# One reload moved forward in an in-order DMA queue: an mLSTM cell followed by a squared-ReLU feed-forward block

## The chip, the cores and the metric

The kernel runs on one core of one Trainium2 chip. The metric is the device time of one execution in microseconds. Faster or slower needs 2%.

## The reference, cut to what matters

```
for t in range(S):                       # 768 steps, 4 x 8 heads of 40
    m_new = max(f_t + m, i_t); C = f*C + i * v_t k_t^T; n = f*n + i*k_t
    y_t = sigmoid(o_t) * (C q_t) / max(|n . q_t|, 1)
x = y as (3072, 320)
out = relu(x @ w_in)**2 @ w_out          # w_in 320 x 2048, w_out 2048 x 320
```

## The kernel before

The sequence is cut into 24 chunks of 128 steps (0 to 23, so "tenth" is chunk 9). Two chunks make a group of 256 rows for the feed-forward block. TensorE works in rounds. A round is the first feed-forward product of group g + 2 (`ffn1_main`, `ffn1_rest`) mixed with the scores and values of two chunks, then the second product of group g (`ffn2_fast`). Everything else is laid around it by hand, in program order: there is no scheduler, and an engine does its instructions in the order of the source.

Three data paths of a chunk go through DRAM, because a reload with another access pattern followed by a 32 x 32 block transpose on VectorE replaces a transpose on TensorE:

```python
def store_num(s):   ... nc.sync.dma_start(n_d[s], tn)            # L557, numerators out
def load_num(s):    ... 4 x nc.sync.dma_start(N, n_d[s, ...])    # L562, and back
def store_rows(s):  ... nc.sync.dma_start(x_d[s], x)             # L613, x out
def load_rows(s):   ... 4 x nc.sync.dma_start(xT, x_d[s, ...])   # L618, and back
def turn_squares(s): nc.vector.transpose(t, t)                   # L625, x ready for TensorE
def pair_up(s):     ... 4 x nc.sync.dma_start(kq_d[s], k or q)   # L287, DRAM to DRAM
def load_squares(s):... 4 x nc.sync.dma_start(kqT, kq_d[s])      # L309, then turn_kq, L316
# (cut) load: k and v, L296; load_o: gates, L324; load_A: 512 KB, L334
```

Numerators are the C q_t of the reference before the division. Squares are k and q of a chunk laid out for 32 x 32 blocks; L309 loads them and L316 turns them for the scores. A is a 512 KB tile from which the weights of the scores are made. A "landing" is the moment when a transfer's data has arrived.

All of these go through one queue, that of SyncE (SP). The output stores of `ffn2_fast` (L779 after its third step, L784 after its fourth) do too. The buffers `y_sb` are three, two per group, so L759 of the next group writes into the buffer that L779 has just sent away.

The order around the tenth chunk (`n` counts quarter rounds, `b` is the chunk number of the round, `r = n % 8`; cut to these lines):

```python
elif r == 1 and g > 1:           # ahead of ffn2_fast
    do(turn_squares, b - 2)
...
elif r == 1:                     # behind ffn2_fast
    if g > 1:
        do(load_rows, b - 1)
        do(pair_up, b + 2)
...
elif r == 5:
    do(store_num, b + 1)
    if b > 9:
        do(load_rows, b)
    do(load_num, b + 1)
elif r == 6:
    if n == 14:
        normalise_turned(9)
        store_rows(9)
    do(load, b + 5)
    for t in range(b + 5, min(b + 7, NT)):
        load_o(t)
    do(load_squares, b + 3)
    if n == 14:
        turn_squares(8)
elif r == 7:
    do(load_A, b + 4)
    if n == 15:
        load_rows(9)
```

## Time and profile before

| | before |
|---|---|
| time, median of the first 3 runs | 533.12 us (532.86 to 534.69) |
| span of the profiled run | 532.4 us |
| TensorE matmul busy | 512.5 us, 96% |
| longest wait of TensorE | 10.7 us, L649 for L625 |

The table is read against its second line: what TensorE does not fill of the span is about 20 us, and one wait is half of it. In the lines that the prediction shows, a row of a timeline gives start, length, engine, source line, operation, output and inputs, count, and in brackets the idle time before it with what ended that. SPq is the sequencer that issues the DMA queue; its length is the time of issue, not of the transfer.

### The profile page before, as it was taken

The numbers are of one execution on the slowest core, as the hardware profiler recorded it, in microseconds if no ns is written. First come the engines' busy times: TensorE is split into PE (matmuls) and PEld (weight loads), VectorE is DVE, ScalarE is ACT, GpSimd is POOL, SyncE is SP. The second block draws the span as 40 slices with busy tenths as digits, with TensorE's granted clock in tenths as the row PEclk, the third lists the DMA queues.
The fourth block names the chain that finished last, engine by engine and source line by source line (L and its number), as shares of the span: only waits on it lengthen the run. The fifth ranks groups of instructions, "written<-read, shape, count | busy, mean of one in ns | idle before, by whom it ended". The sixth has DMA issues, their size and how long they took to land.

```text
span 532.4 us, 10333 instructions
## 1 busy us (share of the span) xinstructions
PE 512.5 (96%) x3933; PEld 449.8 (84%) x3933; DVE 332.3 (62%) x638; ACT 194.2 (36%) x460; POOL 89.9 (17%) x110
## 2 busy tenths in 40 slices
PE   9998999999999946999999999999999999999997
PEld 4876888886898945899898898897898898998997
DVE  8579977869874833556765765564864864441451
ACT  3776586461735210812513704422613301102100
POOL 3346643221221100100110110110210100000000
PEclk9998899999999997999999999999999999999999
DMA  9998698966777685467676766667775121200000
GB/s 192 226 198 205 144 197 178 223 152 142 157 155 146 150 157 108 88 155 140 128 168 130 141 137 129 130 154 144 138 159 104 55 79 50 63 12 1 26 25 26
DMA packets 239394, 68.06 MB, mean 128 GB/s; under 512 B 185744, under 2 KB 233872, under 8 KB 239344
## 3 DMA queue, kind: packets, MB, share of 16 engines
q1 hardware_dynamic: 239248, 67.20, 59.6%
q8 instruction: 31, 0.51, 0.4%
q10 hardware_dynamic: 96, 0.20, 0.1%
q14 instruction: 19, 0.16, 0.1%
HBM read 55.08 MB, written 17.86 MB: 137 GB/s over the span
## 4 chain that ended last, share of the span: by engine, by line
PE 80%; DMA 6%; DVE 6%; SPq 5%; issue 1%; ACT 1%; POOL 0%; DVEq 0%; ACTq 0%
PE h_ps L649 28%; PE h_ps L743 27%; PE h_ps L660 7%; PE tp L424 3%; PE numT L534 3%; PE h_ps L689 2%; DMA num_rows<-tn 2%; DMA x_rows<-x_sb 2%; PE idle L802 2%; PE numT L523 1%; SPq L562 1%; PE hp L460 1%; SPq L309 1%; PE numT L512 1%; SPq L618 1%
## 5 line engine op out<-in xcount | busy, mean ns | idle before, releaser
L649 PE MATMUL h_ps<-xT,w_in 128*128 128x256 f32 x768 | 177.2, 389 | 13.0 <-DVE xT L625 11.6
L649 PEld LDWEIGHTS h_ps<-xT,w_in 128*128 128x128 f32 x768 | 147.0, 194 | 36.4 <-DVE xT L625 12.1
L675 ACT ACTIVATE r_sb<-h_ps 128x512 f32<-128x512 f32 x96 | 50.6, 598 | 121.9 <-issue 63.1
L743 PE MATMUL h_ps<-w_out,g 128*128 128x160 f32 x528 | 76.1, 300 | 0.9 <-DVE y_sb L759 0.9
L743 PEld LDWEIGHTS h_ps<-w_out,g 128*128 128x128 f32 x528 | 72.9, 190 | 1.7 <-DVE y_sb L759 1.4
L682 DVE TENSOR_TENSOR g<-r_sb 128x512 f32<-128x512 f32 x96 | 67.0, 747 | 10.0 <-ACT r_sb L675 10.0
L437 DVE TENSOR_TENSOR P_sb<-tp,W_sb 128x512 f32<-128x512 f32 x46 | 29.6, 684 | 53.4 <-PE numT L534 33.0
L383 ACT ACTIVATE W_sb<-A_bc,b_T 128x128 f32<-128x128 f32 x176 | 53.8, 388 | 22.8 <-POOL A_bc L359 22.7
L743 PE MATMUL h_ps<-T,S 128*128 128x160 f32 x352 | 52.3, 302 | 0.0
L743 PEld LDWEIGHTS h_ps<-T,S 128*128 128x128 f32 x352 | 48.8, 190 | 1.6 <-issue 0.9
L660 PE MATMUL h_ps<-xT,w_in 64*128 64x256 f32 x384 | 49.0, 391 | 0.0
L660 PEld LDWEIGHTS h_ps<-xT,w_in 64*128 64x128 f32 x384 | 34.8, 186 | 12.1 <-issue 9.1
L359 POOL TENSOR_SCALAR_AFFINE_SELECT A_bc<-A_bc 128x1024 f32<-128x1024 f32 x22 | 26.3, 1197 | 83.6 <-ACT kq L369 78.3
L759 DVE TENSOR_TENSOR y_sb<-y_sb,h_ps 128x160 f32<-128x160 f32 x44 | 14.0, 318 | 42.0 <-PE h_ps L743 42.0
L763 ACT COPY y_sb<-h_ps 128x160 f32<-128x160 f32 x11 | 3.2, 293 | 96.4 <-PE h_ps L743 87.4
L396 POOL TENSOR_TENSOR vw<-va,W_sb 128x328 f32<-128x328 f32 x20 | 18.0, 900 | 70.2 <-ACT W_sb L383 52.1
L316 DVE STREAM_TRANSPOSE kqT<-kqT 128x1024 f32<-128x1024 f32 x17 | 21.0, 1237 | 10.3 <-DMA kqT<-kq_rows 10.0
L369 ACT ACTIVATE kq<-A_bc 64x512 f32<-64x512 f32 x30 | 18.8, 628 | 22.2 <-DMA A_bc<-a_rows 20.3
L490 POOL TENSOR_TENSOR Cd<-C,kq 128x164 f32<-128x164 f32 x15 | 7.0, 465 | 117.9 <-DVE C L551 101.9
L424 PEld LDWEIGHTS tp<-kqT 40*128 40x128 f32 x384 | 24.8, 188 | 2.4 <-issue 1.1
L424 PE MATMUL tp<-kqT 40*128 40x128 f32 x384 | 26.1, 275 | 0.0
L743 PE MATMUL h_ps<-w_out,S 128*128 128x160 f32 x176 | 25.7, 299 | 0.0
(119 smaller groups left out, 598.9 us busy)
## 6 DMA issues: line engine op xcount, KB each, us to landing
A_bc<-a_rows SPq DMA_DIRECT2D x23, 512.0 KB, 4.9
raw<-in_moe_w_out_dram SPq DMA_DIRECT2D x16, 320.0 KB, 3.5
num_rows<-tn SPq DMA_DIRECT2D x18, 256.0 KB, 2.6
kq<-num_rows SPq DMA_DIRECT2D x72, 64.0 KB, 2.1
kqT<-kq_rows SPq DMA_DIRECT2D x34, 128.0 KB, 3.0
raw<-in_moe_w_in_dram SPq DMA_DIRECT2D x8, 512.0 KB, 4.5
kq<-in_k_dram SPq DMA_DIRECT2D x24, 160.0 KB, 4.1
va<-in_v_dram SPq DMA_DIRECT2D x24, 160.0 KB, 4.5
```

The lines of the kernel that those rows point to most:

```text
L316: nc.vector.transpose(t, t)
L359: nc.gpsimd.affine_select(A[:], A[:], compare_op=ALU.is_ge, fill=-1e30, base=0, pattern=[[0, H], [1, P]], channel_multiplier=-1,)
L369: nc.scalar.activation(e[rows], st[s]["A"][0][rows, PR * i : PR * (i + 1), :], AF.Exp)
L383: nc.scalar.activation(d["W"][:, i * n + h, :], A[i][:, h, :], AF.Exp, bias=b_T[:, b, c, i * n + h : i * n + h + 1],)
L396: nc.gpsimd.tensor_tensor(d["vw"][:], d["va"][:], d["W"][:, :, P - 1 : P].to_broadcast([P, H, D1]), op=ALU.mult,)
L424: nc.tensor.matmul(sc[i][:, j, :], lhsT=d["kT"][rows, j, :], rhs=d["qT"][rows, j, :], start=True, stop=True,)
L437: nc.vector.tensor_tensor(t, d["sc"][i], d["W"][:, heads, :], op=ALU.mult)
L649: nc.tensor.matmul(hs[i][:, n, :], lhsT=w_in[:, a, fb * P : (fb + 1) * P], rhs=xT[:, :, a, :], start=(n == 0 and a == 0), stop=False,)
L660: nc.tensor.matmul(hs[i][:, n, :], lhsT=w_in2[rows, 2 * pp + n, :], rhs=xT[rows, :, 2, :], start=False, stop=(n == 1),)
L675: nc.scalar.activation(rs[-1][:], h[:], AF.Relu)
L682: nc.vector.tensor_tensor(g4[:, :, i, :], r[:], r[:], op=ALU.mult)
L743: nc.tensor.matmul(to, lhsT=lhsT[:, p], rhs=rhs[:, p, :], start=(start and p == 0), stop=(p == NPAIR - 1), skip_group_check=True,)
```

## The change

Its intent is to send the tenth chunk's x out and back early, so that TensorE no longer waits for it. The store of x now goes ahead of the numerators of the eleventh chunk, and its reload directly behind them. Everything else that stood in between goes behind the reload.

```diff
-        elif r == 1 and g > 1:
+        elif r == 1 and g > 2:
             do(turn_squares, b - 2)
@@
         elif r == 1:
             if g > 1:
+                if g == 2:
+                    turn_squares(9)
                 do(load_rows, b - 1)
@@
             if b > 9:
                 do(load_rows, b)
-            do(load_num, b + 1)
-        elif r == 6:
-            if n == 14:
-                normalise_turned(9)
-                store_rows(9)
+                do(load_num, b + 1)
+        elif r == 6 and b == 9:
+            normalise_turned(9)
+            store_rows(9)
+            load_num(10)
+            load_rows(9)
+            load(14)
+            turn_squares(8)
+        elif r == 7 and b == 9:
+            load_o(14)
+            load_o(15)
+            load_squares(12)
+            load_A(13)
+        elif r == 6:
             do(load, b + 5)
 ...
-            if n == 14:
-                turn_squares(8)
         elif r == 7:
             do(load_A, b + 4)
-            if n == 15:
-                load_rows(9)
```

## The prediction

> **What bounds the kernel now.** I read the page's busy shares and slices first, then what TensorE waited for, the chain of waits around its gap, and the timelines of the DMA queue and of VectorE there.
>
> ```profile
> PE 512.5 (96%) x3933; PEld 449.8 (84%) x3933; DVE 332.3 (62%) x638; ACT 194.2 (36%) x460; POOL 89.9 (17%) x110
> ...
> PE   9998999999999946999999999999999999999997
> ...
> PEclk9998899999999997999999999999999999999999
> ```
>
> TensorE is the bound: over 90% in nearly every slice of 13.3 us. The one hole is the 4 and the 6, and the clock row has its only 7 there. The next view, TensorE's waits, gives the hole one owner:
>
> ```profile
> PE h_ps L649 <- DVE xT L625: 11.6, 2, 10.7
> ```
>
> Two waits, 11.6 us together; one is 10.7 us. No other wait of TensorE exceeds 1.5 us in total. L625 is the block transpose (`turn_squares`) that finishes a chunk's x. In the chain, in order of time, the hole ends so:
>
> ```profile
> 180.76 4.73 DMA num_rows<-tn
> ...
> 188.80 0.38 SPq L613
> ...
> 197.25 0.69 SPq L618
> ...
> 199.01 4.11 DMA xT<-x_rows
> ...
> 203.19 0.59 DVE xT L625
> ...
> 203.83 8.90 PE h_ps L649 x32
> ```
>
> The timeline of the one DMA queue (SP) shows what stands between L613 (store of chunk 9's x) and L618 (its reload):
>
> ```profile
> 185.51 1.74 SPq L562 DMA_DIRECT2D kq<-num_rows  x4
> 187.34 1.36 SPq L779 DMA_DIRECT2D out_dram<-y_sb  x1
> 188.80 0.38 SPq L613 DMA_DIRECT2D x_rows<-x_sb  x1
> 189.28 0.48 SPq L296 DMA_DIRECT2D kq<-in_k_dram  x1
> ...
> 192.20 3.67 SPq L309 DMA_DIRECT2D kqT<-kq_rows  x4
> ...
> 197.25 3.27 SPq L618 DMA_DIRECT2D xT<-x_rows  x4
> ```
>
> On VectorE x was ready at 183.53, when its last copy (L583, 183.33 + 0.20) ended. The store waited until 188.80 because the queue stood at L562, whose data, the numerators of chunk 10, landed only at 185.49. The reload waited to 197.25 behind k and v of chunk 14, gates, squares, an output and a 512 KB A tile. The transpose ended at 203.78. TensorE had finished at 193.17.
>
> **What the Trainium skill says.** "DMA: Bandwidth & Descriptors", section Anatomy of one DMA, says that "DMA engines do not wait on semaphores": the issuing sequencer waits. So a waiting transfer holds up all behind it. The trace agrees: L613 left 5.3 us after its data was ready. The same page, Two DMAs through the same engine are not ordered, says a read of what another DMA wrote must wait for the first one's semaphore, so "straight behind" still includes a landing. Here x stores take 2.1/3.7/6.0 us (least, median, most) from issue to landing. "TensorE: Matmul & The Clock Gate", section Why this matters for your kernels, warns of idle gaps over about 3 us, after which the clock falls. The trace agrees: granted clock 0.68 in 193.2 to 203.8 and 0.80 in 203.8 to 212.7, and 32 matmuls of L649 took 8.90 us there against 7.10 us at 217.1, clock 1.00.
>
> **The change, part by part.** No instruction is added or removed. (a) In the queue, the output store L779 and L613 now precede L562. (b) The reload L618 follows L562 directly, before k, v, gates, squares and A. (c) On VectorE, the transpose of chunk 9 moves behind the last addition (L759) of that stage. Nothing else changes order on an engine; TensorE's order is the same.
>
> Walk, with durations from the rows above and their neighbours. L779's data is ready at 181.82 (L759, 181.50 + 0.32), so it issues near 181.9. L613 issues at 183.6; with the median 3.7 us it lands at 187.3. L562 still waits to 185.49 and ends at 187.25. L618 then takes 187.3 to 189.2 (4 x 0.47, as later reloads do); its last part is issued at 188.75 and lands 2.2 to 3.0 us later (median of all reloads, and of this window), at 191 to 191.8. The earlier L779 also frees the buffer that L759 waited for at 190.35 ("DVE y_sb L759 <- DMA out_dram<-y_sb", 3.2 us), which had cost TensorE 0.57 us. TensorE's four remaining products of 2.17 us, from 183.47, then end at 192.17. L759 runs to 192.53, the transpose to 193.05. **TensorE's next stage starts at T = 193.07 instead of 203.83: 10.76 us earlier**, with 0.9 us of waiting left. At full clock its first 32 matmuls take 7.17 us (as after the 0.96 us wait at 361.28) instead of 8.90: 1.7 us more. Gross gain 12.5 us, or 520.6 us.
>
> **What comes back.** The hole had let the queue run ahead. Moving L618 forward puts an equal amount of issue time in its place: k still issues at about 189.3, and then L784 (0.6 us), gates (1.65), squares (3.6) and A (0.4) put the store of chunk 10's x at about 197.0. In the later rounds that store is issued 0.1, 0.0, 1.5 and 2.1 us after the stage starts (243.95, 282.76, 323.00, 363.35); now it is T + 3.9. From that store to the transpose of the next chunk's k and q (L316) the rounds took 16.2, 16.3, 17.0 and 15.4 us. With 16.0 that is T + 19.9. The round from 321.5, which has the same shape (a sequence starts in it), had L316 at T + 18.5, and there VectorE's addition (L759, 8.6 us later) just met TensorE with 0.02 us to spare. So about 1.2 us of TensorE waiting here.
>
> Further down the same queue, squares end at about 210.4; in the rounds the output store L779 follows 16.6 to 18.9 us later, say 17.4: 227.8, or T + 34.7. It lands 2.1 us later, and L759 needs its buffer, so it runs at T + 36.9. In the 321.5 round the span from that L759 (357.50) to the next L649 (361.28) is 3.8 us, so the next stage starts at T + 40.7, where T + 38.3 would be free of waits (the old 40.0 less 1.7). This loss, 2.4 us, contains the 1.2 us. After it the store is at about 2 us behind the stage start, as at 363.35, which cost nothing. Sum: 12.5 - 2.4 = 10.1, so about 523.0; I take 0.2 us off, because 0.4 us of that loss hangs on an unlucky store landing. **522.8 us**, 1.9% faster.
>
> **The rivals.** (1) Nothing comes back: the queue catches up, as it did from +2.1 us at 363.35 (by 399.48 it was ahead of the stage again). Then 520.6 us. Against it is the round from 321.5, which waited 0.32 and 0.96 us with less lag. (2) The reload lands late, after 192.5: DMA was 83% busy in 193.2 to 203.8, and a reload there took 3.27 us to issue. A delay of 1.5 us moves T and the queue together, giving about 524.5. For it: x stores landed up to 6.0 us late. Against it is the DMA view of 175 to 245 us, in 40 slices of 1.75 us:
>
> ```profile
> DMA  6436932379999796154287000498469352589997
> ```
>
> The sixth to eighth slices (183.75 to 189) are 3, 2 and 3 tenths busy, so the moved transfers run in free time. (3) The wait is replaced by another of equal size, so that almost nothing is gained: VectorE standing at the transpose with relu squares behind it, or L316 of chunk 12 late. Its squares now land near 199.3, its transpose ends near 200.6, and TensorE needs it at T + 9.1 = 202.2. VectorE is 62% busy, so a loss above 5 us looks unlikely; it would give 526 or more.
>
> **Range and chances.** The 2% line is at 522.5, nearly in the middle of what I expect, so the class is uncertain. Queue landings vary by 1 to 2 us, and the loss may be anything from 0 to 5. Low 520.5, high 525.2. Faster by over 2%: 0.42; within 2%: 0.57; slower: 0.01.
>
> **What would show it.** Right: L618 issued at 187 to 188; the L649 wait of 10.7 us down to about 1; 32 matmuls back near 7.1 us; clock row without the 7; L613 of chunk 10 near 197; L316 late near T + 20 and a wait of L743 or L649 of 1 to 3 us in total before 236. Wrong: a stage start after 195 (rival 2), no new waits (rival 1), or a new TensorE wait above 4 us (rival 3). A slower kernel would need VectorE or the queue to delay TensorE by over 20 us; nothing in the walk does.

## The result, and the profile after

The changed kernel took 525.8 us in the median of 4 runs (524.81 to 528.05), against 532.99 us (530.7 to 534.69) of the kernel before. The ratio is 0.9874, with a 95% interval of 0.9825 to 0.9923. Ratios here are the mean time of one kernel's fast runs over that of the other's in the same rounds, so not quite the ratio of the medians. That is a real gain, but within 2%, and 0.6 us above the range that was forecast.

The page of the changed kernel, its busy shares and slices:

```profile
PE 511.7 (98%) x3933; PEld 448.5 (86%) x3933; DVE 333.2 (64%) x638; ACT 194.4 (37%) x460; POOL 90.4 (17%) x110
...
PE   9998999999999999989999999999999999999997
...
PEclk9998899999999999999999999999999999999999
```

The 4 and the 6 of TensorE and the 7 of its clock are gone. What TensorE waited for at L649 and L743 in the whole span (total, times, longest):

```profile
PE h_ps L649 <- DVE xT L625: 3.2, 3, 1.4
...
PE h_ps L743 <- DVE y_sb L759: 0.9, 3, 0.5
```

The wait of 10.7 us is gone, but L649 now waits three times and L743 three times. The timeline of TensorE shows four of them:

```profile
192.63 7.17 PE L649 MATMUL h_ps<-xT,w_in 128*128 128x256 f32 x32 [0.90 <-DVE xT L625]
...
220.30 2.44 PE L743 MATMUL h_ps<-w_out,S 128*128 128x160 f32 x16 [0.15 <-DVE y_sb L759]
...
229.79 2.44 PE L743 MATMUL h_ps<-w_out,g 128*128 128x160 f32 x16 [0.53 <-DVE y_sb L759]
233.62 6.74 PE L649 MATMUL h_ps<-xT,w_in 128*128 128x256 f32 x30 [1.39 <-DVE xT L625]
```

The stage after the old hole starts at 192.63 with 0.9 us of waiting, and its 32 matmuls take 7.17 us instead of 8.90. Then waits come that the kernel before did not have in this round. (The last row is cut by the end of the view, at 240 us.) The queue, in the same stretch:

```profile
181.01 0.35 SPq L779 DMA_DIRECT2D out_dram<-y_sb  x1
182.72 0.37 SPq L613 DMA_DIRECT2D x_rows<-x_sb  x1
183.31 1.76 SPq L562 DMA_DIRECT2D kq<-num_rows  x4
185.17 1.91 SPq L618 DMA_DIRECT2D xT<-x_rows  x4
...
195.25 0.83 SPq L613 DMA_DIRECT2D x_rows<-x_sb  x1
199.86 1.86 SPq L618 DMA_DIRECT2D xT<-x_rows  x4
...
206.54 2.59 SPq L309 DMA_DIRECT2D kqT<-kq_rows  x4
...
227.33 0.38 SPq L779 DMA_DIRECT2D out_dram<-y_sb  x1
```

The first four lines are the change: the reload leaves at 185.17, not 197.25. The fifth is the store of chunk 10's x, 2.6 us after the stage start, and the reload behind it leaves 4.6 us later, when the store has landed. What that leads to is on VectorE:

```profile
211.67 1.25 DVE L316 STREAM_TRANSPOSE kqT<-kqT 128x1024 f32<-128x1024 f32 x1 [5.77 <-DMA kqT<-kq_rows]
...
229.41 0.33 DVE L759 TENSOR_TENSOR y_sb<-h_ps,y_sb 128x160 f32<-128x160 f32 x1 [5.10 <-DMA out_dram<-y_sb]
```

VectorE stood 5.8 us for the squares of chunk 13 and 5.1 us for the output store. Three rounds later in the same trace it stands at the same two places again:

```profile
330.68 1.25 DVE L316 STREAM_TRANSPOSE kqT<-kqT 128x1024 f32<-128x1024 f32 x1 [5.95 <-DMA kqT<-kq_rows]
...
348.09 0.33 DVE L759 TENSOR_TENSOR y_sb<-h_ps,y_sb 128x160 f32<-128x160 f32 x1 [4.64 <-DMA out_dram<-y_sb]
```

In the SP queue's own waits between 176 and 240 us the largest is the one for stores of x to land:

```profile
SPq L618 <- DMA x_rows<-x_sb: 10.7, 3, 3.7
```

**One table for all runs.** Times of single runs scatter by some 3 us to either side (528.31 to 535.38 us for before in the timed calls), and between traces the reference start below moves by as much (150.9 to 154.2). So I compare stage starts inside a trace. Each stage start is the first L649 row of a group's first product. The reference is the start of the round before the hole (153.25 us in the first trace). *a* runs from there to the start behind the hole (T, 203.83 in that trace), *b* is the next round (to T2, 243.67), *c* the three rounds after it (to 361.28). After that, the first traces of both kernels take the same time to the end, 171.1 us. A start with no wait ahead of it reads up to 0.16 us earlier than one behind a wait.

| trace | a | b | c | a + b + c |
|---|---|---|---|---|
| before, mean of 5 | 50.32 (48.91 to 51.46) | 40.26 | 118.10 | 208.7 |
| after, mean of 3 | 40.27 (40.08 to 40.39) | 41.58 | 119.41 | 201.3 |
| before, the 2 fast ones | 50.26 | 40.05 | 117.40 | 207.7 |
| after, the 2 fast ones | 40.36 | 40.84 | 118.61 | 199.8 |
| reload_only | 41.52 | 42.68 | 119.96 | 204.2 |
| nums_only | 47.55 | 40.87 | 117.98 | 206.4 |
| turn_first | 39.49 | 42.33 | 119.99 | 201.8 |
| y1_on_act | 40.35 | 38.65 | 118.26 | 197.3 |
| outs_og_act | 42.26 | 39.48 | 119.61 | 201.4 |
| before_fill, two traces | 47.49, 48.97 | 38.01, 38.12 | 115.86, 117.62 | 201.4, 204.7 |
| pairs_first | 40.55 | 38.12 | 115.85 | 194.5 |
| pairs_y1 | 40.56 | 38.11 | 115.86 | 194.5 |
| pairs_y1_turn | 39.49 | 38.09 | 115.86 | 193.4 |

Without any wait, then, b is 38.1 and c is 115.9 us: several different kernels arrive at exactly these. Three of the five traces of before and one of the three of after are of single runs of unknown state. By the fast traces alone the change gains 9.9 us in a and loses 0.8 us in b and 1.2 us in c, 7.9 us in sum; with all traces it is 10.05, 1.3 and 1.3, 7.4 in sum. The gain in a is far outside the scatter. The loss in c is not: c is 117.2 to 119.8 us in the five traces of before and 118.3 to 121.0 in the three of after. What is clear is that in both kernels these rounds take longer than 115.9.

### The profile page after: what moved, and what is told of

It reads as the page before. It is cut to its first block, busy times and chain, and to the rows that moved or that the text cites. A ratio compares the mean times of both kernels' runs of the same rounds, so it can differ in the third digit from the quotient of the medians.

```text
span 523.0 us, 10336 instructions
## 1 busy us (share of the span) xinstructions
PE 511.7 (98%) x3933; PEld 448.5 (86%) x3933; DVE 333.2 (64%) x638; ACT 194.4 (37%) x460; POOL 90.4 (17%) x110
## 4 chain that ended last, share of the span: by engine, by line
PE 78%; DMA 8%; DVE 7%; SPq 4%; issue 1%; ACT 1%; POOL 0%; DVEq 0%; ACTq 0%
PE h_ps L743 27%; PE h_ps L649 25%; PE h_ps L660 7%; DMA x_rows<-x_sb 4%; PE tp L424 3%; PE h_ps L689 3%; PE numT L534 2%; DVE g L682 2%; PE hp L460 2%; PE idle L802 2%; DMA kqT<-kq_rows 1%; PE numT L523 1%; SPq L618 1%; SPq L562 1%; DMA kq_rows<-in_q_dram 1%
## 5 line engine op out<-in xcount | busy, mean ns | idle before, releaser
L649 PE MATMUL h_ps<-xT,w_in 128*128 128x256 f32 x768 | 175.6, 386 | 4.5 <-DVE xT L625 3.2
L649 PEld LDWEIGHTS h_ps<-xT,w_in 128*128 128x128 f32 x768 | 145.7, 193 | 27.9 <-DVE xT L625 4.2
L743 PE MATMUL h_ps<-w_out,g 128*128 128x160 f32 x528 | 76.0, 300 | 0.6 <-DVE y_sb L759 0.5
L743 PEld LDWEIGHTS h_ps<-w_out,g 128*128 128x128 f32 x528 | 72.9, 190 | 1.4 <-DVE y_sb L759 1.1
L743 PE MATMUL h_ps<-T,S 128*128 128x160 f32 x352 | 52.4, 302 | 0.0
L743 PEld LDWEIGHTS h_ps<-T,S 128*128 128x128 f32 x352 | 48.7, 190 | 1.8 <-issue 1.1
L759 DVE TENSOR_TENSOR y_sb<-y_sb,h_ps 128x160 f32<-128x160 f32 x44 | 13.9, 317 | 40.2 <-PE h_ps L743 40.0
L359 POOL TENSOR_SCALAR_AFFINE_SELECT A_bc<-A_bc 128x1024 f32<-128x1024 f32 x22 | 27.6, 1253 | 66.4 <-ACT kq L369 62.0
L316 DVE STREAM_TRANSPOSE kqT<-kqT 128x1024 f32<-128x1024 f32 x17 | 21.1, 1240 | 15.9 <-DMA kqT<-kq_rows 15.7
L424 PEld LDWEIGHTS tp<-kqT 40*128 40x128 f32 x384 | 24.9, 188 | 2.7 <-issue 1.4
L424 PE MATMUL tp<-kqT 40*128 40x128 f32 x384 | 26.6, 276 | 0.0
L743 PE MATMUL h_ps<-w_out,S 128*128 128x160 f32 x176 | 25.9, 300 | 0.4 <-DVE y_sb L759 0.4
```

The lines of the kernel that those rows point to most:

```text
L359: nc.gpsimd.affine_select(A[:], A[:], compare_op=ALU.is_ge, fill=-1e30, base=0, pattern=[[0, H], [1, P]], channel_multiplier=-1,)
L424: nc.tensor.matmul(sc[i][:, j, :], lhsT=d["kT"][rows, j, :], rhs=d["qT"][rows, j, :], start=True, stop=True,)
L649: nc.tensor.matmul(hs[i][:, n, :], lhsT=w_in[:, a, fb * P : (fb + 1) * P], rhs=xT[:, :, a, :], start=(n == 0 and a == 0), stop=False,)
L743: nc.tensor.matmul(to, lhsT=lhsT[:, p], rhs=rhs[:, p, :], start=(start and p == 0), stop=(p == NPAIR - 1), skip_group_check=True,)
```

## The experiments

**The two kernels again.** Unchanged files, for the scatter.

> The kernel before, unchanged, for a second trace and for the spread. Theory S (the shortfall of the prediction is scatter of single runs: the first trace of before was a slow run, that of after a fast one): ratio to before 0.998 to 1.002, but the wait of L649 anywhere from 8.5 to 11.5 us and the stage start anywhere within 2 us of 203.8. Rival F (the first trace is typical, and the after kernel loses more in most runs than in its trace): the wait again 10.2 to 11.2 us and the span within 1 us of 532.4.

Measured: 532.66 us, ratio 0.9983 (0.9923 to 1.0042), TensorE's wait 9.47 us, start at 203.71. Theory S allows all of it; rival F's wait of 10.2 to 11.2 us is missed, though the span, 532.3 us, is as it said.

> The changed kernel, unchanged, in five rounds. Prediction's size: ratio 0.981 (10.1 us less). First measurement: 0.9874 (6.7 us less). Theory S: near 0.985 (about 8 us), with the stage starts T about 192 to 194 and T2 about T + 41 as in the first trace. Rival F: ratio 0.987 or above, and a trace with waits of TensorE after 190 us of 5 us or more in total, against 4.2 us in the first trace.

Measured: 525.73 us, ratio 0.9864 (0.9825 to 0.9903). So the first ratio was no accident. It lies between what S and F gave. In this trace TensorE waits 3.5 us in all after 190 us, less than F's 5; a is 40.39, b 40.69.

**The two moves apart.** The reload alone goes forward, the numerators stay in front:

```diff
-                do(load_num, b + 1)          # behind "if b > 9"
+            do(load_num, b + 1)
@@
             store_rows(9)
-            load_num(10)
             load_rows(9)
```

> The reload of chunk 9's x is straight behind its store as in the changed kernel, but the numerators of chunk 10 stay ahead of both, as before. Theory Q (each us that the reload leaves earlier is a us of TensorE's hole, until the next stage's other needs): store at 188.8, reload near 191.5 to 192.5, stage start near 196.5 to 197.5, so some 4 us later than in the changed kernel; ratio about 0.992 to 0.995. Rival W (where the numerators stand does not matter): as the changed kernel, within 1 us.

Measured: 529.78 us, ratio 0.9943 (0.9894 to 0.9991). The queue of this run:

```profile
185.59 1.74 SPq L562 DMA_DIRECT2D kq<-num_rows  x4
187.43 0.38 SPq L779 DMA_DIRECT2D out_dram<-y_sb  x1
187.90 1.82 SPq L613 DMA_DIRECT2D x_rows<-x_sb  x1
191.42 1.85 SPq L618 DMA_DIRECT2D xT<-x_rows  x4
...
200.69 0.68 SPq L613 DMA_DIRECT2D x_rows<-x_sb  x1
```

The total is as theory Q said, but not its place. The reload leaves 4 to 5 us later than in the fast traces of the changed kernel (counted from the reference start), yet a is only 1.2 us longer, because the reload of the changed kernel has time to spare. The other 3.2 us (204.2 - 199.8 - 1.2, one trace against the two fast ones) are lost in b and c: the queue now stands idle between 189.7 and 191.4 for the store to land, and the store of chunk 10's x is 5.1 us behind the stage start. In the changed kernel the numerators fill that dead time; by this one trace, that is a good part of what their move is worth.

The numerators alone go back, the reload stays behind A:

```diff
             store_rows(9)
             load_num(10)
-            load_rows(9)
             load(14)
@@
             load_A(13)
+            load_rows(9)
```

> Only the numerators move behind the store; the reload stays behind k, v, the output, gates, squares and A, as before. Theory Q: reload near 195.5, stage start near 201 to 202, so 2 to 3 us better than before, ratio 0.993 to 0.997. Rival W': the place behind gates and squares is all that matters, so the reload leaves at 197 as before and the ratio is 1.000.

Measured: 531.84 us, ratio 0.9974 (0.9925 to 1.0023), which the time alone cannot tell from nothing. In the trace the reload leaves at 193.52, 41.7 us after the reference start against 44.0 in the first trace of before, and a is 47.55. That looks like the 2 to 3 us of theory Q, but one trace cannot show it: in the first trace of `before_fill` below, where the queue has its old order, the reload left 41.3 us after the reference start and a was 47.49. So Q against W' stays open here.

**Is it TensorE's waits, or the queue?** The 0.9 us left at T is the transpose queued behind the last addition. It goes back ahead of it:

```diff
-        elif r == 1 and g > 2:
+        elif r == 1 and g > 1:
             do(turn_squares, b - 2)
@@
             if g > 1:
-                if g == 2:
-                    turn_squares(9)
```

> The changed kernel with the transpose of chunk 9 ahead of the stage's last addition on VectorE again, as before the change (the reload has landed by then). The 0.9 us wait of L649 at the stage start T must vanish in any theory. Theory Q (the next stage start T2 is set by the DMA queue, through the output store L779 whose buffer L759 needs): the queue does not move, so T2 stays 41.2 us after the third L649 row (the stage start of the round before), the 0.9 us comes back as a longer wait before T2, and the ratio is that of the changed kernel, 0.986. Rival E (TensorE's waits simply add up): T2 and the end are 0.9 us earlier, ratio 0.9845.

Measured: 526.14 us, ratio 0.9864 (0.983 to 0.9897), that of the changed kernel. T came 0.8 us earlier (a 39.49), b took it all back:

```profile
192.20 7.07 PE L649 MATMUL h_ps<-xT,w_in 128*128 128x256 f32 x32
...
215.11 1.25 PE L424 MATMUL tp<-kqT 40*128 40x128 f32 x16 [2.36 <-issue]
```

L424 is the scores of chunk 13, which need the transpose L316; it ran from 213.76 after 8.4 us of waiting for its squares. (The view names no releaser for the 2.36 us; L424 reads the tile that L316 had just turned.) (The "41.2 us" of the expectation is a slip for 81.2, which is a + b; it measured 81.8.) Theory Q's core holds: here a gain at T that the queue could not follow was worth nothing. Its detail fails: the path back was L316, not L779.

**Past the queue.** The output store L779 goes to ScalarE's queue:

```diff
             add(m1, m1, Y)
             t = g * GT + 1
-            nc.sync.dma_start(out[t * P : (t + 1) * P, :], y1[:])
+            nc.scalar.dma_start(out[t * P : (t + 1) * P, :], y1[:])
```

> The changed kernel with the first output store of each stage (L779) issued from ScalarE's queue, so that it no longer stands behind the reloads and numerators in the SP queue. Theory Q: the 5 us wait of L759 for the output store goes, the waits of 0.5 and 1.4 us of TensorE near 230 and 233 fall below 0.5 us in total, and so does the one of 0.96 us near 352; T2 1.5 to 2 us earlier, the end 2 to 3 us earlier, ratio about 0.981. Rival L (it is the late transpose L316 of k and q, not L779, that sets T2): no change at T2 within 0.5 us, ratio 0.986.

Measured: 523.74 us, ratio 0.9843 (0.9807 to 0.9878). b fell to 38.65, 2.2 us below the fast traces of the changed kernel, and at T2 there is no wait at all. So in this round of the changed kernel L779 is what set T2. But c is still 118.26: in the next round L316 came 19.7 us after the stage start, and the additions queued behind it made TensorE wait:

```profile
261.48 2.44 PE L743 MATMUL h_ps<-w_out,S 128*128 128x160 f32 x16 [1.04 <-DVE y_sb L759]
```

There x had been stored at 234.92, 3.3 us behind the stage start, and its reload left only at 240.56. So Q and L are both half right: the same late queue has two ways to TensorE, and closing one leaves the other.

The other output store and the gates follow L779 to ScalarE's queue:

```diff
+            # L784, and load_o of chunks 14 and up
-            nc.sync.dma_start(...)
+            nc.scalar.dma_start(...)
```

> As y1_on_act, and the other output store (L784) and the gates (L324) from ScalarE's queue too, which takes about 2.9 us of issue time per stage off the SP queue. Theory Q (the queue's lag is what comes back): the store of chunk 10's x leaves within 1 us of T, L316 no longer waits 5 to 6 us but under 3, the rounds to 352 take 38.3 and 38.9 us with no wait of TensorE above 0.3 us except that at T; end 3 to 4 us earlier than the changed kernel, ratio 0.979. Rival B (the transfers' bandwidth, not their place in the queue, sets the lag): landings get later by as much, and the ratio is that of y1_on_act or worse.

Measured: 527.51 us, ratio 0.9895 (0.9864 to 0.9927; one of its six runs, 534.57 us, was over 1.5% above the fastest), no better than the changed kernel and behind `y1_on_act`. The number is the one that rival B gave. The queue of this run:

```profile
184.88 0.36 SPq L613 DMA_DIRECT2D x_rows<-x_sb  x1
185.34 4.79 SPq L562 DMA_DIRECT2D kq<-num_rows  x4
190.23 2.80 SPq L618 DMA_DIRECT2D xT<-x_rows  x4
```

ScalarE issued L784 and both gates between 186.7 and 188.3, and meanwhile the four numerator loads took 4.79 us to issue instead of 1.76, so the urgent reload left 5.3 us after its store instead of 2.5. In the chain of this trace the last of the four loads is issued at 189.83, right behind the landing of the gates. VectorE then stood 2.4 us for these numerators (L574), ahead of the transpose that TensorE waits for, and a grew by 2 us. So the transfers in the second queue got in the way of more urgent ones of the first; whether by bandwidth or by something else, this run does not tell.

**Filling the dead time.** The four pair copies wait for nothing. They go between the store of x and its reload, in every round:

```diff
-                do(load_rows, b - 1)
                 do(pair_up, b + 2)
+                do(load_rows, b - 1)
```

> The changed kernel, with the four pair copies (L287) of each stage issued before instead of after the reload of x (L618) that waits 4 to 6 us for its store. Nothing else moves. Theory D (what comes back is dead time of the one in-order queue, standing at L618 for a store to land, and it can be filled): in the first round squares leave near T + 10.5 to 11.5 instead of T + 14, L316 no longer waits 5.8 us but under 3.5, T2 about 1.5 to 2 us earlier, the round ending near 352 loses its wait of 0.96 us; end 2 to 3.5 us earlier than the changed kernel, ratio 0.980 to 0.983. Rival B (bandwidth): the pair copies and the store slow each other, squares leave no earlier, ratio 0.986 as the changed kernel.

Measured: 520.68 us, ratio 0.9772 (0.9736 to 0.9807): better than theory D's range. The interval reaches to 1.9%, so the 2% of a verdict is not certain (class: unclear). The queue of this run:

```profile
198.33 0.53 SPq L613 DMA_DIRECT2D x_rows<-x_sb  x1
198.91 1.20 SPq L287 DMA_DIRECT2D kq_rows<-in_k_dram  x2
200.15 1.23 SPq L287 DMA_DIRECT2D kq_rows<-in_q_dram  x2
203.05 1.86 SPq L618 DMA_DIRECT2D xT<-x_rows  x4
205.02 3.35 SPq L309 DMA_DIRECT2D kqT<-kq_rows  x4
```

The store of x is even later than in the changed kernel (T + 4.3), and still the squares leave 6.7 us behind it instead of 11.3 (206.54 - 195.25). The waits of VectorE shrink or vanish:

```profile
210.73 1.25 DVE L316 STREAM_TRANSPOSE kqT<-kqT 128x1024 f32<-128x1024 f32 x1 [3.43 <-DMA kqT<-kq_rows]
...
228.06 0.33 DVE L759 TENSOR_TENSOR y_sb<-h_ps,y_sb 128x160 f32<-128x160 f32 x1 [2.95 <-PE h_ps L743]
```

L316 is at T + 16.7, and L759 waits for TensorE again, not for a store. From there to the end TensorE waits for nothing; b and c are 38.12 and 115.85 us. Three rounds later L316 has no wait any more, and L759 waits for TensorE there too:

```profile
343.91 0.33 DVE L759 TENSOR_TENSOR y_sb<-h_ps,y_sb 128x160 f32<-128x160 f32 x1 [2.95 <-PE h_ps L743]
```

Rival B falls: DMA had room, the queue's order had not. The swap took two waits off the queue at once. Between 190 and 352 us, L618 had waited 25.4 us for stores of x in the first trace of the changed kernel, and waits 9.7 us here; L309 had waited 5.3 us for the pair copies to land (2.2 us of it before 206.54), and does not wait here. No run separates the two.

> pairs_first and y1_on_act together (output store L779 from ScalarE's queue as well). Theory D: both take from the same loss of 2.5 us in the first round and 1 us in the later ones, so they do not add: 0.979 to 0.982. Rival: they add, 0.977 or lower.

Measured: 519.46 us, ratio 0.9767 (0.9731 to 0.9803; class: unclear). The number is the one that the rival named, 0.977 or lower, but only because `pairs_first` alone was already at 0.9772. b and c are the same as there to 0.01 us, so the two do not add.

> pairs_y1 with the transpose of chunk 9 in its old place ahead of L759, which took 0.9 us off T and gave nothing at T2 while the queue set T2. Theory D: with the queue's dead time filled the 0.9 us reaches the end, ratio 0.0015 below pairs_y1. Rival: the queue still sets T2 and the ratio is that of pairs_y1.

Measured: 519.3 us in 5 runs, ratio 0.9763 (0.973 to 0.9797), the only one of the three that is clearly faster by 2%. The traces show the gain at T now staying (a + b + c 193.4 against 194.5), as theory D said; the times are too close to tell these three apart. All three beat both kernels. The plain swap `pairs_first` gives nearly all of it.

**The clock's part by itself.** The kernel before, with zero matmuls in the hole:

```diff
         elif r == 1:
+            if g == 2:
+                idle(36)      # 36 bf16 matmuls 128 x 512 of zeros
             if g > 1:
```

> The kernel before, with 36 matmuls of zeros filling about 8 us of TensorE's 10 us hole; results unchanged. It measures the clock's part by itself. Theory of the prediction: the clock stays up, the 32 matmuls after the hole take 7.1 to 7.2 us instead of 8.9, and the end is 1.7 us earlier, ratio 0.9968. Rival: the slow matmuls after the hole cost nothing in the end, because later waits for the queue take the 1.7 us back: ratio 1.000 although the 32 matmuls are fast.

Measured: 528.99 us, ratio 0.9909 (0.9862 to 0.9955), from few runs that scattered from 525.58 to 535.19 us (the last over 1.5% above the fastest).

```profile
190.51 8.04 PE L802 MATMUL idle<-zeros 128*128 128x512 bf16 x36
```

The next 32 matmuls took 7.07 us and b was 38.01. In this trace the rounds happened to be quicker in a and c as well.

> before_fill once more, with five rounds: its first measurement (0.9909, three rounds scattered over 10 us) gave more than the clock's 1.7 us (0.9968). Theory S (scatter): 0.994 to 0.998, the stage start near 50 us after the third L649 row as in the two traces of before, the next at 38.0 us after it. Rival: the fill also shortens something else, ratio 0.992 or below again, and the trace shows where.

Measured: 532.13 us, ratio 0.9983 (0.9943 to 1.0022); 7.17 us for the 32 matmuls, b 38.12, a 48.97, c 117.62. The trace gives the clock's part: b is 40.26 in the mean of five traces of before and 38.0 to 38.1 with the hole filled, so 2.1 us. It is all in the first 32 matmuls behind the hole: they took 8.83 to 10.02 us in the five traces of before, 9.31 in the mean, against 7.17. The times, 0.9909 and 0.9983, do not agree well enough to give it.

**Was the hole of the first trace a typical one?** More traces of the same files, one run each, of unknown state; only intervals inside them are used.

> A third trace of the kernel before, to see how long the hole is in a typical run. From the third L649 row (stage start of the round before) to the stage start after the hole: 50.6 and 49.9 us in its two traces so far, 47.5 and 49.0 in the two traces of before_fill, whose queue is the same up to there. Theory S (the first trace, from which the prediction took the hole, was an extreme one): below 50.3. Rival: the traces of before_fill are the odd ones, 50.0 to 50.7.

> A fourth trace of the kernel before, as before_t3. Theory S: below 50.3, mean of all five or six traces near 49.3. Rival: 50.0 to 50.7.

> A fifth trace of the kernel before, as before_t3. Theory S: below 50.3. Rival: 50.0 to 50.7.

Measured: a is 51.46, 48.91 and 50.70 (times 536.68, 535.63 and 535.51 us, beside 535.57 us of the kernel before on that chip). Theory S falls: the mean of five is 50.32, and the first trace, 50.58, was an ordinary one.

> A third trace of the changed kernel. The stage start T came 40.3 and 40.4 us after the third L649 row in its two traces, the next one 81.3 and 81.1, the one near 352 199.6 and 200.0. If the change also removes the scatter of the hole (the reload has landed before TensorE needs it), T is again 40.2 to 40.6; if not, it varies by 1 us or more as in the kernel before.

Measured: a is 40.08, b 43.05, c 121.01 (530.99 us). So a is within 0.3 us in three traces, where it spread over 2.6 us before: the reload is ahead of its need. What scatters now is b and c, by 2.4 and 2.8 us.

## Why the prediction was wrong

The forecast was 10.3 us less. In the terms of the table that was 10.76 in a, a loss of 0.7 in b (1.7 for the clock, less 2.4), nothing in c, and 0.2 us added by hand. The fast traces gave 9.9, a loss of 0.8 and a loss of 1.2: 7.9 us (7.4 with all traces). The two timed calls gave 6.7 and 7.3 us (1 - 0.9874 and 1 - 0.9864, of 533).

- **What bounds the kernel, and what the change does: right.** The wait of 10.7 us went, the reload left at 185.2, earlier than the 187 to 188 forecast, the matmuls are at 7.17 us, the 7 in the clock row is gone.
- **The start T: 0.9 us too good by the fast traces (0.7 by all).** 0.3 is the first trace against the mean of before. The rest is in the walk: it put the end of TensorE's products 38.9 us after the reference start, and they end at 39.4 (191.73 - 152.30).
- **The clock: right, slightly small.** 1.7 forecast, 2.1 measured by the fill. The 8.90 us of the first trace were the second shortest of five.
- **"What comes back", in the first round: right in kind, and in the fast traces in size.** T2 at "T + 40.7" was 40.99 and 40.69. Part of that is luck. L779 came at T + 34.7 as forecast, but the squares ended 0.8 us earlier (T + 16.5) and L779 followed them 0.8 us later (18.2 us) than assumed; and the store of chunk 10's x left at T + 2.6, not T + 3.9. In the third trace, a single run of unknown state, the store left at T + 4.9, L316 came at T + 21.1 and T2 at T + 43.05.
- **The step that failed is the one after it:** "After it the store is at about 2 us behind the stage start, as at 363.35, which cost nothing." The lag came as forecast (2.0 and 2.5 us behind T2 in the fast traces), but it was not free: the next three rounds took 118.25 and 118.96 us where `pairs_first` takes 115.85, and 1.2 us more than in the fast traces of before. Most of this is in the third of these rounds: 40.3 us in both fast traces of the changed kernel, 39.3 and 39.8 in those of before, 38.0 in `pairs_first`. It is a round in which a sequence starts, of the same shape as the first. The prediction had read the waits of 0.32 and 0.96 us in it in the kernel before, and yet carried no cost over. Read from one round of one trace, "cost nothing" missed that even the kernel before lost 1.5 us in these rounds (117.40 against 115.86), at the same two places (L316 waited 5.3 us and L759 4.9 us in its first trace). `pairs_first`, which takes only waits off the queue, removes the loss. That the change itself adds 1.2 us to it is not clear of the scatter between traces.
- **"I take 0.2 us off"** was taken in the wrong direction.
- **The rivals.** The late reload of rival 2, the catching-up of rival 1 and the new wait above 4 us of rival 3 did not happen; the longest new wait of TensorE was 1.4 us. The upper end of the range left 4.6 us of the gross 12.5 for everything that comes back. The timed calls leave 5.2 to 5.8, with the shortfall at T in it.

## What to carry to other kernels

In this in-order queue, an item that waited for another transfer to land cost the queue that time (10.7 us between 176 and 240 us), whoever needed what stood behind. Before moving an urgent transfer forward, look for where the queue stands idle and put independent transfers there; here that swap of two lines gave another 5 us on top of the change, with all the later rounds in it. And when a hole on the bound engine is closed, check what the hole had been hiding: the slack of the feeding queue in the following rounds, from several traces.

## What the Trainium skill lacked or had wrong

- "DMA: Bandwidth & Descriptors", section Issuing engines are not separate DMA queues, says that initiating DMAs from several engines only saves issue time on the sequencer, "usually small relative to the DMA itself". It leaves out an item waiting ahead: taking one 160 KB store out of the SP queue cut a round from 40.7 to 41.0 us, in the fast traces, to 38.7 us (`y1_on_act`). That such transfers interleave on the same engines fits: with gates and outputs on ScalarE's queue, four 64 KB loads took 4.79 us to issue instead of 1.76 (`outs_og_act`).
- The same page, section Anatomy of one DMA, gives a fixed part of about 2 us (fitted for the path through GpSimd, not this one). The section has no figure for landing behind a busy queue. Here a 192 KB store of x behind a 512 KB tile held its reload back by 3.95 to 6.33 us, counted from issue to issue at the round starts of the fast traces of the changed kernel.
- No page says what an in-order queue costs when one item waits for a landing, or that filling that wait is a remedy: three rounds of 118.3 and 119.0 us became 115.85 (c, the fast traces of the changed kernel and `pairs_first`).
- "TensorE: Matmul & The Clock Gate", section Why this matters for your kernels, names the gap of about 3 us; the traces agree (a gap of 2.72 us left the next 32 matmuls at 7.17 us in `outs_og_act`, one of 8.01 us made them 9.92 us in `nums_only`) and add the price of one gap of 9 to 11 us: 2.1 us, in the first product behind it.
